# A smaller edge tile on 64x64 quadrants, mixer bursts joined in pairs, and their transposes moved: a change to a gated-attention and mixer kernel

## The chip, the cores and the metric

The kernel runs on one core of one Trainium2 chip. The metric is the device time of the whole program in microseconds (us), median of several runs. The engines are called as the profile calls them: PE is TensorE (PEld its weight loads), ACT is ScalarE, DVE is VectorE, POOL is GpSimd, SP is SyncE. SP only issues DMA transposes here.

## The reference, cut to what matters

There are 8 batches of S = 3136 rows; u and v have 256 columns, z has 64, the rank is 32.

```python
scores = (1.0 / S) * np.matmul(z, z.transpose(0, 2, 1))
x = u * np.matmul(np.maximum(scores, 0.0) ** 2, v)        # attention part
h = x.transpose(0, 2, 1) @ U @ V                           # low rank, along the rows
u2 = x + h.transpose(0, 2, 1)
out = u2 + np.maximum(u2 @ w_ch1, 0.0) @ w_ch2             # channel mixer, 256 -> 1024 -> 256
```

3136 rows are 24 tiles of 128 and one of 64, which is tile 24.

## The kernel before

The squared scores A are symmetric. So the kernel computes for each row tile j only 13 of 25 blocks (in `A[j]`) and gets the other 12 by a DMA transpose into a `strip`, issued four outputs ahead. An "output" is one row tile of the attention result. They are done in pairs that share a set of two PSUM banks, in the order 12, 13, ..., 24, 0, ..., 11; below, "output i" is the i-th place in this order, counted from 0, and tile 24 is output 12. Two 64-row matmuls at a time work on the two row halves of the array:

```python
def half(b, o, j, h, w, start, stop, **kw):
    ...
    mm(out=acc[t0][h][:, (o - t0) * D : (o - t0 + 1) * D],
       lhsT=w[halves[h]], rhs=v_both[b % 2][halves[h], j, :], ...)

def close_pair(b, o):
    ...
    nc.scalar.copy(out=both[:, :w], in_=banks[1][:, :w])
    nc.vector.tensor_tensor(out=both[:, :w], in0=banks[0][:, :w], in1=both[:, :w], op=ALU.add)
    nc.vector.tensor_tensor(out=x_at(b, t0, n), ..., op=ALU.mult)      # times u
```

Tile 24 has only 64 rows. Its z is stored twice over, so its 128 columns hold the same 64 rows twice, and half of its matmul work is wasted.

The mixer of batch b-1 runs inside the attention of batch b. There are 7 chunks of two to four row tiles. For each, `low_rank` puts a sum into the PSUM set that the open pair is not using, DVE adds it to x, and SP transposes the result into `ut`. A "burst" n then runs the up matmuls of chunk n (evicted by ACT with relu) and the down matmuls of chunk n-1:

```python
def low_rank(b, c, ps=None):
    ps = spare() if ps is None else ps          # the set that no open pair uses
    ... mm(...)                                  # four matmuls
    nc.vector.tensor_tensor(out=q, in0=split(ps[h]...), in1=q, op=ALU.add)   # twice
    transpose(out=ut..., in_=x...)               # SP queue

# the loop over the outputs of one batch, cut
burst_at = dict(zip((2, 4, 6, 8, 10, 13, 15, 17), range(NC + 1)))
z_load, z_double, z_half, z_turn = (1, 5, 7, 11) if b else (None, 9, 11, 13)
ahead = dict(zip((1, 2, 4, 6, 8, 10, 13), range(NC)))
for i in range(begin, NT):
    fill = [...]                                 # scores, spread over the output's matmuls
    if i == z_turn:     turn_z(b + 1, ((0, FIRST),))      # z of the next batch, SP queue
    if i == z_turn + 1: extend_z()                        # a DVE copy of what was turned
    main = attend_steps(b, o)
    if b and i in ahead:
        main.insert(NT * 2 // 5, lambda c=ahead[i]: low_rank(b - 1, c))      # step 10 of 25
    _spread(main, fill)
    if i + AHEAD < NT:  turn(b, turns(i + AHEAD))         # a strip, SP queue
    ...
    if b and i in burst_at:
        up, down = bursts[burst_at[i]]
        run(_merge(down, up))
```

`turn_z` overwrites z, so it can only start after the last score of the running batch (output 10 before).

Of the kernel before, what the change touches and what calls it, by code (L numbers as in the profile page):

```python
# [10 lines left out]
ALU = mybir.AluOpType  # L11
# [3 lines left out]
def _ceil_div(a, b):  # L15
    return (a + b - 1) // b
# [15 lines left out]
def _merge(*lists):  # L32

    keyed = [
        ((i + 0.5) / len(part), n, s)
        for n, part in enumerate(lists)
        for i, s in enumerate(part)
    ]
    return [s for _, _, s in sorted(keyed, key=lambda e: e[:2])]
# [3 lines left out]
def kernel(  # L43
# [11 lines left out]
    nc = tc.nc  # L55

    B, S, D = u.shape
# [4 lines left out]
    NT = _ceil_div(S, P)  # L62
    NF = S // P
# [8 lines left out]
    FIRST = HALF  # L72
# [22 lines left out]
    halves = [slice(h * ROWS, (h + 1) * ROWS) for h in range(2)]  # L95
# [5 lines left out]
    def spare():  # L101

        return sets[(opened[0] + (0 if acc else 1)) % 2]
# [4 lines left out]
    mm = nc.tensor.matmul  # L108
# [9 lines left out]
    v_both = [persist.tile([P, NT, D], BF16, name=f"v{k}") for k in range(2)]  # L118
# [4 lines left out]
    def turns(i):  # L123
        return (FIRST + i) % NT
# [4 lines left out]
    def col(t):  # L129
        return place(t) * P  # L130
# [10 lines left out]
    NC = len(chunks)  # L141
# [7 lines left out]
    def x_at(b, t, n=1):  # L149

        c, k = offset[t]
        return group(b, c)[:, :, k : k + n, :].rearrange("p a t c -> p t a c")

    def split(ap):
        return ap.rearrange("p (t a c) -> p t a c", a=ND, c=P)
# [32 lines left out]
    def extend_z():  # L188
        nc.vector.tensor_copy(out=zT[:, NT:, :], in_=zT[:, :HALF, :])
# [114 lines left out]
    acc = {}  # L304
    u_tiles = {}

    def pair_of(o):
        first = 0 if o < FIRST else FIRST
        stop = FIRST if o < FIRST else NT
        t0 = o - (o - first) % 2  # L310
        return t0, min(2, stop - t0)
# [11 lines left out]
    def open_pair(b, o):  # L323
        acc[pair_of(o)[0]] = sets[opened[0] % 2]
        opened[0] += 1

    def block(b, o, j):
        k = (o - j) % NT
        return A[j][:, k * P : (k + 1) * P] if k <= HALF else strips[b, o][:, NT - 1 - k, :]
# [12 lines left out]
    def close_pair(b, o):  # L342
        t0, n = pair_of(o)
        banks, u_sb = acc.pop(t0), u_tiles.pop((b, t0))
        w = n * D
        both = both_pool.tile([P, 512], FP32, name="both")
        nc.scalar.copy(out=both[:, :w], in_=banks[1][:, :w])  # L347
        nc.vector.tensor_tensor(  # L348
            out=both[:, :w], in0=banks[0][:, :w], in1=both[:, :w], op=ALU.add
        )  # L350
        nc.vector.tensor_tensor(  # L351
            out=x_at(b, t0, n),
            in0=split(both[:, :w]),
            in1=u_sb[:, :n, :].rearrange("p t (a c) -> p t a c", c=P),
            op=ALU.mult,
        )

    def after(b, o):

        t0, n = pair_of(o)  # L360
        i = place(t0) + n
        return (b, turns(i)) if i < NT else (b + 1, turns(0))

    def attend_steps(b, o):
        t0, n = pair_of(o)
        last = t0 + n - 1
        js = [(o - k) % NT if k < NB else (o + k - HALF) % NT for k in range(NT)]
        js.remove(NF)

        def step(i):  # L370
            if i == 0 and o == t0:
                open_pair(b, o)
                if after(b, o)[0] < B:
                    load_u(*after(b, o))
            if i < NT - 1:
                w = block(b, o, js[i])
                end = i == NT - 2
                half(b, o, js[i], 0, w, i == 0, end and o > t0)
                half(b, o, js[i], 1, w, i == 0 and o == t0, end)
            elif o == t0:  # L380
                half(b, o, NF, 0, block(b, o, NF), False, True)
                if o < last:
                    half(b, o + 1, NF, 1, block(b, o + 1, NF), True, False)
            if i == NT - 1 and o == last:
                close_pair(b, o)

        return [lambda i=i: step(i) for i in range(NT)]
# [26 lines left out]
    def low_rank(b, c, ps=None):  # L414

        ts = chunks[c]
        ps = spare() if ps is None else ps
        where = [(0, 0), (1, 0)] if len(ts) == 2 else [(0, 0), (0, 1), (1, 0), (1, 1)]
        order = sorted(zip(where, ts), key=lambda e: (e[0][1], e[0][0]))
        for (h, k), t in order:  # L420
            mm(  # L421
                out=ps[h][:, k * D : (k + 1) * D],
                lhsT=V_bf[halves[h], col(t) : col(t) + P],
                rhs=t1[b][halves[h], :],
                start=True,
                stop=True,
            )
        n = len(ts)
        x = group(b, c)
        dst = x.rearrange("p a t c -> p t a c")  # L430
        for h in range(2):
            ks = [k for (g, k), _ in zip(where, ts) if g == h]
            k0 = len(ks) * h if n == 2 else 2 * h
            q = dst[:, k0 : k0 + len(ks)]
            nc.vector.tensor_tensor(out=q, in0=split(ps[h][:, : len(ks) * D]), in1=q, op=ALU.add)  # L435
        ut = ut_pool.tile([P, ND * 512], BF16, name="ut")
        ut = ut[:, : ND * n * P].rearrange("p (a w) -> p a w", a=ND)
        transpose(
            out=ut.rearrange("p a (t c) -> p (a t) c", c=P),
            in_=x.rearrange("p a t c -> p (a t c)"),  # L440
        )
        uT[c] = ut
# [211 lines left out]
    own_at = {i: [] for i in range(NT)}  # L654
    for i, j in enumerate(range(LEAD + NG - 1, NT)):
        own_at[i].append((j, 0, NB))
    for j, i in enumerate((6, 7, 8, 9, 10, 10, 4, 2, 9, 8, 7, 6)):
        own_at[i].append((j, 0, FIRST - j))


# [11 lines left out]
    def run(steps):  # L672
        for s in steps:
            s()
# [4 lines left out]
    late = []  # L679
    for b in range(B):  # L680
        more = b + 1 < B
        begin = 0 if b else 2 * NG
        bursts = bursts_of(b - 1) if b else []
        burst_at = dict(zip((2, 4, 6, 8, 10, 13, 15, 17), range(NC + 1)))
        z_load, z_double, z_half, z_turn = (1, 5, 7, 11) if b else (None, 9, 11, 13)
        soon = next_at if b else next_first
        v_at = (1, 3, 4, 5, 7, 8, 10, 11, 12) if b else (8, 9, 10, 12, 14, 15, 16, 17, 18)
        v_at = dict(zip(v_at, V_PARTS))
        ahead = dict(zip((1, 2, 4, 6, 8, 10, 13), range(NC)))
        first = []  # L690
        if b == 0:
            for j, k1 in [(NT - 1, NB)] + [(j, NB if j < 3 else FIRST - j) for j in range(FIRST)]:
                first += score_steps(j, 0, k1)
        for i in range(begin, NT):
            o = turns(i)
            fill = []
            if b == 0:
                if i < z_turn:
                    n = _ceil_div(len(first), z_turn - i)
                    fill, first = first[:n], first[n:]  # L700
            else:
                fill = [s for key in own_at[i] for s in score_steps(*key)]
            if more:
                fill += [s for key in soon[i] for s in score_steps(*key)]
                if i == z_load:
                    load_z(b + 1, WHOLE)
                if i == z_double:
                    double_z(b + 1, WHOLE)
                if i == z_half:
                    turn_z(b + 1, ((FIRST, NF),))  # L710
                if i == z_turn:
                    turn_z(b + 1, ((0, FIRST),))
                if i == z_turn + 1:
                    extend_z()
                if i in v_at:
                    load_v(b + 1, v_at[i])
            main = attend_steps(b, o)
            if b and i in ahead:
                main.insert(NT * 2 // 5, lambda c=ahead[i]: low_rank(b - 1, c))
            _spread(main, fill)  # L720
            if i + AHEAD < NT:
                turn(b, turns(i + AHEAD))
            elif more:
                turn(b + 1, turns(i + AHEAD - NT))
            if b == 0 and i in weights:
                weights[i]()
            if b and i == 0:
                rank(b - 1)
            if b and i in burst_at:
                up, down = bursts[burst_at[i]]  # L730
                if not more and burst_at[i] >= NC - 1:
                    late += up + (down if burst_at[i] == NC else [])
                    up, down = [], (down if burst_at[i] < NC else [])
                run(_merge(down, up))


    last = bursts_of(B - 1)
# [5 lines left out]
    for c in range(NC + 1):  # L743
        up, down = last[c]
        if c + 2 < NC:
            up = up[:1] + [lambda c=c: low_rank(B - 1, c + 2, other)] + up[1:]
# [30 lines left out]
```

## Time and profile before

The median was 1065.91 us. The profiled run spans 1063.6 us.

| what | value | read from |
|---|---|---|
| PE busy, DVE, ACT | 95%, 49%, 57% | page, busy times |
| one batch, start to start of the rank matmuls | 126.83 us | timeline of PE |
| a slot: 2 matmuls of 64 rows x 256 columns, or one full-array of 256 | 109 ns | timeline of PE |
| excess over these slots in one batch | 5.4 us, once 5.8 and once 7.1 | worked out from matmul starts |
| a switch between 64-row and full-array matmuls | 0.09 to 0.10 us | worked out from matmul starts |

"Excess" is the time from one matmul start to the next on the same part of the array minus the slot (109 ns for 256 columns, 216 ns for 512).

The page's busy times and the chain that ended last:

```profile
PE 1010.7 (95%) x13829; PEld 791.3 (74%) x13829; DVE 525.3 (49%) x937; ACT 611.4 (57%) x814; POOL 178.7 (17%) x332
...
PE 81%; DVE 7%; ACT 5%; issue 3%; DMA 2%; POOL 1%; SPq 0%; POOLq 0%; ACTq 0%; DVEq 0%
```

PE is the bottleneck, and DMA is 2% of the chain: in the steady batches PE waits for a transfer only once (1.7 us, for a `ut`, in the one long period). Three lines of the waits (who waited for whom: us in total, times, longest) say the same:

```profile
DVE zT L189 <- DMA zT<-z_bf: 13.6, 2, 10.7
...
PE ps L421 <- DVE both L348: 8.3, 28, 0.4
...
PE ps L455 <- DMA ut<-x_bf: 4.3, 2, 2.7
```

L421 is the low-rank sum waiting for its PSUM set. L189 is the DVE copy of z; both its waits are in the first batch. The mixer waited for a `ut` only twice, once in the tail.

The timeline of PE shows tile 24 (start, duration, instruction): 24 slots, 2.63 us to the next output at 442.28.

```profile
439.65 1.47 PE L333 MATMUL ps<-v,A 64*128 64x256 bf16 x24
440.96 1.47 PE L333 MATMUL ps<-v,strip 64*128 64x256 bf16 x24
```

The timeline of the SP queue around the turning of z in the same batch:

```profile
431.19 1.23 SPq L438 DMA_TRANSPOSE ut<-x_bf  x1
432.52 1.48 SPq L295 DMA_TRANSPOSE strip<-A  x1
434.08 3.42 SPq L184 DMA_TRANSPOSE zT<-z_bf  x1
437.59 4.84 SPq L295 DMA_TRANSPOSE strip<-A  x2
```

### The profile page before, as it was taken

The numbers are of one execution on the slowest core, as the hardware profiler recorded it, in microseconds if no ns is written. First come the engines' busy times: TensorE is split into PE (matmuls) and PEld (weight loads), VectorE is DVE, ScalarE is ACT, GpSimd is POOL, SyncE is SP. The second block draws the span as 40 slices with busy tenths as digits, with TensorE's granted clock in tenths as the row PEclk, the third lists the DMA queues.
The fourth block names the chain that finished last, engine by engine and source line by source line (L and its number), as shares of the span: only waits on it lengthen the run. The fifth ranks groups of instructions, "written<-read, shape, count | busy, mean of one in ns | idle before, by whom it ended". The sixth has DMA issues, their size and how long they took to land.

```text
span 1063.6 us, 31097 instructions
## 1 busy us (share of the span) xinstructions
PE 1010.7 (95%) x13829; PEld 791.3 (74%) x13829; DVE 525.3 (49%) x937; ACT 611.4 (57%) x814; POOL 178.7 (17%) x332
## 2 busy tenths in 40 slices
PE   5879999999999999999999999999899999999896
PEld 4667777787777867788677877788677787778564
DVE  4858554465544654456543555436444465432331
ACT  5857555566645665466655665646665566541253
POOL 4122112111121111211121121211112110111011
PEclk9999999999999999999999999999999999999998
DMA  9999989779897998959899898987989797588231
GB/s 173 183 195 179 174 165 173 168 159 171 167 164 158 174 173 170 179 139 163 162 174 178 152 170 163 165 183 145 173 155 172 158 170 136 125 149 162 62 100 64
DMA packets 417174, 168.71 MB, mean 159 GB/s; under 512 B 392768, under 2 KB 402640, under 8 KB 417040
## 3 DMA queue, kind: packets, MB, share of 16 engines
q1 hardware_dynamic: 386464, 96.77, 56.9%
q0 software_dynamic: 30576, 69.96, 27.1%
q8 instruction: 108, 1.77, 0.7%
q14 instruction: 26, 0.21, 0.1%
HBM read 61.88 MB, written 25.69 MB: 82 GB/s over the span
## 4 chain that ended last, share of the span: by engine, by line
PE 81%; DVE 7%; ACT 5%; issue 3%; DMA 2%; POOL 1%; SPq 0%; POOLq 0%; ACTq 0%; DVEq 0%
PE ps L333 43%; PE ps L486 16%; PE ps L455 15%; PE ps L260 6%; ACT A L273 3%; DVE x_bf L435 3%; DVE both L348 2%; DVE A L275 2%; DMA zT<-z_bf 1%; PE ps L401 1%; DVE x_bf L351 1%; ACT both L347 1%; PE ps L421 1%; ACT relu L462 1%; DMA ut<-x_bf 1%
## 5 line engine op out<-in xcount | busy, mean ns | idle before, releaser
L273 ACT ACTIVATE A<-ps 128x832 bf16<-128x832 f32 (+8 forms) x469 | 351.7, 763 | 176.4 <-PE ps L260 170.6
L333 PE MATMUL ps<-v,A 64*128 64x256 bf16 x5064 | 358.6, 271 | 5.7 <-DVE x_bf L435 2.3
L275 DVE TENSOR_TENSOR A<-A 128x832 bf16<-128x832 bf16 (+8 forms) x469 | 240.3, 524 | 209.8 <-ACT A L273 206.8
L333 PE MATMUL ps<-v,strip 64*128 64x256 bf16 x4612 | 319.9, 270 | 0.0
L462 ACT ACTIVATE relu<-ps 128x1024 bf16<-128x1024 f32 (+2 forms) x224 | 203.1, 916 | 186.0 <-PE ps L455 186.0
L333 PEld LDWEIGHTS <-A 64*128 64x128 bf16 x5064 | 251.7, 94 | 64.5 <-issue 27.1
L333 PEld LDWEIGHTS <-strip 64*128 64x128 bf16 x4612 | 233.2, 94 | 34.1 <-issue 0.2
L455 PE MATMUL ps<-ut,w_bf 128*128 128x512 bf16 (+2 forms) x896 | 204.4, 354 | 7.4 <-DMA ut<-x_bf 4.3
L486 PE MATMUL ps<-w_bf,relu 128*128 128x256 bf16 x1600 | 205.9, 273 | 1.0
L486 PEld LDWEIGHTS <-relu 128*128 128x128 bf16 x1600 | 153.8, 98 | 49.5 <-issue 9.3
L497 DVE TENSOR_TENSOR o_sb<-ps,x_bf 128x512 f32<-128x512 f32 (+1 forms) x104 | 69.7, 670 | 221.3 <-PE ps L486 221.3
L260 PE MATMUL ps<-zT 64*128 64x416 bf16 (+9 forms) x933 | 156.0, 318 | 18.4 <-DMA zT<-z_bf 15.8
L455 PEld LDWEIGHTS <-w_bf 128*128 128x128 bf16 x896 | 86.3, 98 | 65.6 <-issue 11.6
L317 POOL DMA_DIRECT2D u_sb<-in_u_dram x96 | 53.5, 558 | 474.4 <-DVE x_bf L351 436.0
L504 POOL DMA_DIRECT2D out_dram<-o_sb x96 | 52.4, 546 | 330.2 <-DVE o_sb L497 330.2
L348 DVE TENSOR_TENSOR both<-ps,both 128x512 f32<-128x512 f32 (+1 forms) x104 | 69.3, 666 | 55.4 <-ACT both L347 55.0
L347 ACT COPY both<-ps 128x512 f32<-128x512 f32 (+1 forms) x104 | 58.9, 567 | 63.0 <-PE ps L333 63.0
L260 PEld LDWEIGHTS <-zT 64*128 64x128 bf16 x933 | 53.0, 95 | 27.2 <-DMA zT<-z_bf 16.1
L435 DVE TENSOR_TENSOR x_bf<-ps,x_bf 128x512 bf16<-128x512 f32 (+1 forms) x112 | 65.4, 626 | 14.7 <-PE ps L421 14.6
L351 DVE TENSOR_TENSOR x_bf<-both,u_sb 128x512 bf16<-128x512 f32 (+1 forms) x104 | 69.8, 671 | 3.6
L195 POOL DMA_DIRECT2D v<-in_v_dram x61 | 34.1, 566 | 0.5 <-issue 0.5
L421 PE MATMUL ps<-t_sb,V_bf 64*128 64x256 bf16 x200 | 22.6, 273 | 9.9 <-DVE both L348 8.3
(33 smaller groups left out, 134.0 us busy)
## 6 DMA issues: line engine op xcount, KB each, us to landing
u_sb<-in_u_dram POOLq DMA_DIRECT2D x96, 256.0 KB, 3.5
out_dram<-o_sb POOLq DMA_DIRECT2D x96, 256.0 KB, 3.0
v<-in_v_dram POOLq DMA_DIRECT2D x57, 192.0 KB, 5.7
strip<-A SPq DMA_TRANSPOSE x196, 4.9
z_c<-in_z_dram POOLq DMA_DIRECT2D x7, 384.0 KB, 5.7
w_bf<-in_moe_w_ch_dram POOLq DMA_DIRECT2D x2, 512.0 KB, 8.5
u_sb<-in_u_dram POOLq DMA_DIRECT2D x16, 64.0 KB, 2.1
ut<-x_bf SPq DMA_TRANSPOSE x56, 3.4
```

What stands on the lines that cost most here:

```text
L260: mm(out=ps[:, k, :n], lhsT=zT[halves[k], j, :], rhs=zT_flat[halves[k], c : c + n], start=True, stop=True,)
L273: nc.scalar.activation(out=dst, in_=src, func=AF.Relu, scale=sc)
L275: nc.vector.tensor_tensor(out=dst, in0=dst, in1=dst, op=ALU.mult)
L333: mm(out=acc[t0][h][:, (o - t0) * D : (o - t0 + 1) * D], lhsT=w[halves[h]], rhs=v_both[b % 2][halves[h], j, :], start=start, stop=stop, **kw,)
L347: nc.scalar.copy(out=both[:, :w], in_=banks[1][:, :w])
L348: nc.vector.tensor_tensor(out=both[:, :w], in0=banks[0][:, :w], in1=both[:, :w], op=ALU.add)
L351: nc.vector.tensor_tensor(out=x_at(b, t0, n), in0=split(both[:, :w]), in1=u_sb[:, :n, :].rearrange("p t (a c) -> p t a c", c=P), op=ALU.mult,)
L435: nc.vector.tensor_tensor(out=q, in0=split(ps[h][:, : len(ks) * D]), in1=q, op=ALU.add)
L455: mm(out=ps[:, i, :w], lhsT=w1_bf[:, db, (hp + i) * P : (hp + i + 1) * P], rhs=uT[c][:, db, len(chunks[c]) * P - w :], start=(db == 0), st ...
L462: nc.scalar.activation(out=relus[c][:, hp : hp + 2, :w], in_=ps[:, :, :w], func=AF.Relu)
L486: mm(out=ps[:, k * D : (k + 1) * D], lhsT=relus[c][:, ht, q : q + P], rhs=w2_bf[:, ht, :], start=(ht == 0), stop=(ht == NH - 1),)
L497: nc.vector.tensor_tensor(out=o_sb[:p, :nk, :].rearrange("p t (a c) -> p t a c", c=P), in0=split(ps[:p, : nk * D]), in1=x_at(b, t, nk)[:p] ...
```

## The change

The intent: halve the matmuls of tile 24, halve the number of switches into and out of the mixer, and place the low-rank sums where their PSUM set is already free. Within a burst, up now comes before down. The core of the diff:

```diff
+        if o == NF:                                   # in close_pair: fold the two column halves
+            for r in range(2):
+                nc.scalar.copy(out=both[halves[r], w : 2 * w], in_=both[halves[1 - r], :w])
+            nc.vector.tensor_tensor(
+                out=both[:, :w], in0=both[:, :w], in1=both[:, w : 2 * w], op=ALU.add
+            )
 ...
+    def quarter(b, j, n, h):
+        c = n % 2
+        mm(
+            out=acc[NF][h][halves[c], :D],
+            lhsT=block(b, NF, j)[halves[h], halves[c]],
+            rhs=v_both[b % 2][halves[h], j, :],
 ...
-    for j, i in enumerate((6, 7, 8, 9, 10, 10, 4, 2, 9, 8, 7, 6)):
+    for j, i in enumerate((6, 7, 8, 9, 3, 5, 4, 2, 9, 8, 7, 6)):
 ...
-        burst_at = dict(zip((2, 4, 6, 8, 10, 13, 15, 17), range(NC + 1)))
-        z_load, z_double, z_half, z_turn = (1, 5, 7, 11) if b else (None, 9, 11, 13)
+        burst_at = {4: (0, 1), 8: (2, 3), 13: (4, 5), 17: (6, 7)}
+        z_load, z_double, z_half, z_turn = (1, 5, 7, 10) if b else (None, 9, 11, 13)
 ...
-        ahead = dict(zip((1, 2, 4, 6, 8, 10, 13), range(NC)))
+        ahead = dict(zip((2, 3, 6, 7, 10, 11, 14), range(NC)))
 ...
-                main.insert(NT * 2 // 5, lambda c=ahead[i]: low_rank(b - 1, c))
+                main.insert(14 if (i + (i > FIRST)) % 2 == 0 else 8, lambda c=ahead[i]: low_rank(b - 1, c))
 ...
-                run(_merge(down, up))
+                run(_merge(up, down))                 # for both bursts n of burst_at[i]
```

Two row tiles j share a slot: the even ones go to the first 64 output partitions, the odd ones to the other 64, and the two halves are added at the end.

More of the change, by code (lines that the diff above doesn't have):

```diff
@@ L355, in close_pair @@
             op=ALU.mult,
+        )
+    def quarter(b, j, n, h):
[4 more added lines that the diff above has]
+            rhs=v_both[b % 2][halves[h], j, :],
+            start=(n < 2),
+            stop=(n == (NT - 2 if c else NT - 1 - 2 * h)),
         )
@@ L374, in step @@
                     load_u(*after(b, o))
-            if i < NT - 1:
+            if o == NF:
+                if i < NT - 1 and i % 2:
+                    for n in (i - 1, i):
+                        for h in range(2):
+                            quarter(b, js[n], n, h)
+                elif i == NT - 1:
+                    quarter(b, NF, i, 0)
+            elif i < NT - 1:
                 w = block(b, o, js[i])
@@ L728 @@
                 rank(b - 1)
-            if b and i in burst_at:
-                up, down = bursts[burst_at[i]]
-                if not more and burst_at[i] >= NC - 1:
-                    late += up + (down if burst_at[i] == NC else [])
-                    up, down = [], (down if burst_at[i] < NC else [])
-                run(_merge(down, up))
+            for n in burst_at.get(i, ()) if b else ():
+                up, down = bursts[n]
+                if not more and n >= NC - 1:
+                    late += up + (down if n == NC else [])
+                    up, down = [], (down if n < NC else [])
+                run(_merge(up, down))
     last = bursts_of(B - 1)
```

## The prediction

> **What bounds the kernel now.** TensorE. The page shows PE busy 95% of 1063.6 us and 81% of the chain that ended last; ACT (57%) and DVE (49%) are no limits. The batches repeat every 126.83 us (start to start of the rank matmuls in the timeline; one period is 128.56). Matmul by matmul, the timeline shows slots of 109 ns for a pair of 64-row matmuls of 256 columns or a full-array one of 256, and 216 ns for 512. Over these slots, a period has only 4.0 us of excess:
> - low-rank sums (L421) waiting for a spare PSUM set: 1.84 us;
> - an output's opening (L333) waiting for a set that a low-rank sum still holds: 0.59 us;
> - entering and leaving 8 mixer bursts: 16 switches of 0.09 to 0.10 us, 1.5 us, and 0.3 us in two entries, where down waits for PSUM;
> - the first, up-only burst waiting for relu evictions (1.02 us each against 0.87 us of matmuls): 0.54 us.
>
> **What the change does, per period.**
> 1. Quadrants: output tile 24 takes 24 slots, 2.63 us. Four 64x64 matmuls at once need 12: -1.31 us. The rank matmuls (128x32) start as four every 100 to 110 ns, so I expect four per slot. The Trainium skill (TensorEngine Tiling, "Key Properties" and "Restrictions") says that a change of tiling mode drains the array and that column tiling loses the fast weight load; the trace agrees on the first (0.09 us per switch); that 64-column loads stay hidden is a guess. Two switches cost 0.19. Net -1.1. The added ACT copies (2 x about 0.37) and DVE add (about 0.42) lie behind the close, off the chain.
> 2. Double bursts: eight switches fewer, -0.76; entry stalls gone, -0.3; but burst 1 now follows the up-only burst at once: one more wait for an eviction, +0.25.
> 3. Low-rank sums: step 14 comes 1.5 to 1.9 us after the opening, the set is free at about 1.7 to 1.9. But two sums in adjacent outputs put 2.8 us more on DVE in 6.5 us, so the second sum and the next opening still wait 0.3 to 0.4 in places. Of 2.4 us I expect 1.1 to stay: -1.3.
> 4. z sooner: the last own scores are now in output 9, and the DVE copy that extends zT stands at the start of output 11, with no burst between. Turning z takes 3.4 to 8.0 us from issue to landing. DVE is in order, so it is blocked 1 to 2 us and the opening of tile 24 is late by about 0.6 (0 to 1.5), in six batches.
>
> Sum: about -2.6 us per batch, seven batches: -18.5. First batch: quadrants alone, broken by scores: -0.5. The single 1.8 us wait for ut in the long period probably goes: -1. The start and the tail of about 70 us are unchanged. All this is on the critical path, since PE is.
>
> **Predicted: 1045 us, 80% range 1037 to 1054.** Faster by over 2%: 0.46; within 2%: 0.53; slower: 0.01.
>
> **What would show it.** A period near 124.2 us. Quadrant matmuls in fours every 105 to 115 ns. Four burst entries and four exits of about 0.09 us. Stalls before low-rank sums under half of 1.84 us. A wait of DVE's zT copy for DMA in the steady batches, which has none before; then a late opening of tile 24.
>
> **What would make it wrong.** Quadrants not four at once (slots of 160 to 210 ns): +5 to +9 us. No waits on DVE or zT: 1036. The longer burst-free stretch (12 outputs instead of 10, DMA share already 0.94 there) making strips late: several us more.

## The result, and the profile after

The changed kernel takes 1052.58 us (four runs, 1050.61 to 1056.54), the kernel before 1066.2 us in the same rounds. The ratio is 0.9878, with a 95% interval of 0.9847 to 0.991. A ratio here is the mean time of one kernel's fast runs over that of the other's of the same rounds, so not quite the ratio of the medians. The profiled run spans 1050.1 us, 13.5 less than before. Note the scatter: 5.9 us between the changed kernel's runs, 2.3 us between those of before.

The line numbers move by 24 in the mixer: L421 is now L445 (low-rank matmul), L455 is L479 (up), L486 is L510 (down), L435 is L459. The page of the changed kernel:

```profile
PE 996.5 (95%) x13829; PEld 788.7 (75%) x13829; DVE 527.8 (50%) x945; ACT 616.8 (59%) x830; POOL 179.2 (17%) x332
...
PE 77%; DMA 10%; ACT 4%; issue 3%; DVE 3%; POOL 1%; SPq 0%; POOLq 0%; ACTq 0%; DVEq 0%
```

PE is busy 14 us less, as it should be. But the share of DMA in the chain that ended last went from 2% to 10%: transfers now set the pace in places. The waits of the changed kernel:

```profile
DVE zT L189 <- DMA zT<-z_bf: 22.3, 8, 11.7
...
ACT A L273 <- DMA strip<-A: 12.8, 5, 3.8
...
PE ps L479 <- DMA ut<-x_bf: 6.8, 9, 2.7
...
PE ps L367 <- DVE x_bf L459: 2.3, 6, 0.8
```

The line of low-rank sums waiting for `both` (8.3 us, 28 times before) has gone. But this view leaves out idle times under 150 ns, and it counts from the modelled ends of matmuls. By the matmul starts, the sums still wait 1.0 us in a period, where they waited 1.9, and the waits of an opening behind a sum (0.6) have gone. Three waits for DMA have come or grown: of the mixer for `ut`, of ACT for strips (before there was none of this kind), and of DVE for z in every batch that has a next one. The last line is tile 24 (L367) waiting for the adds of a low-rank sum, which stand on DVE behind the copy of z.

Tile 24, timeline of PE of the changed kernel: 1.54 us from its first matmul to the next output's at 429.84, where it was 2.63.

```profile
428.30 0.85 PE L367 MATMUL ps<-v,A 64*64 64x256 bf16 x24
428.98 0.82 PE L367 MATMUL ps<-v,strip 64*64 64x256 bf16 x24
429.64 0.27 PE L367 MATMUL ps<-v,A 64*64 64x256 bf16 x1
```

The SP queue of the changed kernel in the same batch:

```profile
422.08 1.61 SPq L184 DMA_TRANSPOSE zT<-z_bf  x1
425.84 1.24 SPq L462 DMA_TRANSPOSE ut<-x_bf  x1
427.17 4.15 SPq L295 DMA_TRANSPOSE strip<-A  x1
431.41 1.26 SPq L462 DMA_TRANSPOSE ut<-x_bf  x1
432.76 7.94 SPq L295 DMA_TRANSPOSE strip<-A  x3
```

Now z stands in front of the `ut` and the strip, six us before tile 24 opens. The strip issued at 427.17 then delays something else. Here is the chain that ended last in that window (start, duration, what):

```profile
426.63 0.54 PE ps L333 x10
427.17 8.50 DMA strip<-A
...
435.75 0.39 ACT A L273
436.15 0.04 issue
436.19 1.02 PE ps L479 x4
```

And the timeline of ACT of the changed kernel at the same place (the bracket is idle time and what ended it):

```profile
431.66 0.28 ACT L273 ACTIVATE A<-ps 128x128 bf16<-128x128 f32 x1
435.75 0.38 ACT L273 ACTIVATE A<-ps 128x256 bf16<-128x256 f32 x1 [3.82 <-DMA strip<-A]
436.03 1.02 ACT L486 ACTIVATE relu<-ps 128x1024 bf16<-128x1024 f32 x1
```

The 128x256 score belongs to the next batch. It overwrites row 1 of A and must wait until that row's strip has landed. Behind it in ACT's queue stand the relu evictions of the double burst that has begun meanwhile, and so PE stops inside the burst: in this batch for 1.68 us.

The excess over the slots, summed over the seven periods between the first and the eighth group of rank matmuls (882.93 us before, 868.05 us after), gives this account. All rows are worked out from the matmul starts of the two profiled runs, each start against the end of the slot before it on the same part of the array; "forecast" is the prediction's term times its number of batches.

| term | forecast, us | measured, us |
|---|---|---|
| tile 24: slots, and its two switches | -7.7 | -7.3 |
| low-rank sums and openings waiting for PSUM | -9.1 | -10.7 |
| burst switches, and entries waiting for PSUM or ACT | -7.4 | -8.3 |
| relu evictions at the first up burst | +1.8 | +2.4 |
| opening of tile 24 late, behind the copy of z on DVE | +3.6 | +3.1 |
| bursts waiting for `ut` (1.7 before, 4.3 after) | -1 | +2.6 |
| PE stopped in the burst by ACT waiting for a strip | none | +3.3 |
| up to the first rank matmuls (116.0 to 117.4 us) | -0.5 | +1.4 |
| after the last ones (64.7 and 64.6 us) | 0 | 0.0 |

The measured column adds up to -13.5, as much as lies between the two spans.

### The profile page after: what moved, and what is told of

It reads as the page before. It is cut to its first block, busy times and chain, and to the rows that moved or that the text cites. A ratio compares the mean times of both kernels' runs of the same rounds, so it can differ in the third digit from the quotient of the medians.

```text
span 1050.1 us, 31112 instructions
## 1 busy us (share of the span) xinstructions
PE 996.5 (95%) x13829; PEld 788.7 (75%) x13829; DVE 527.8 (50%) x945; ACT 616.8 (59%) x830; POOL 179.2 (17%) x332
## 4 chain that ended last, share of the span: by engine, by line
PE 77%; DMA 10%; ACT 4%; issue 3%; DVE 3%; POOL 1%; SPq 0%; POOLq 0%; ACTq 0%; DVEq 0%
PE ps L333 41%; PE ps L510 15%; PE ps L479 13%; PE ps L260 6%; DMA ut<-x_bf 4%; DMA strip<-A 3%; DMA zT<-z_bf 3%; ACT A L273 3%; PE ps L425 1%; ACT relu L486 1%; PE ps L445 1%; DVE A L275 1%; DVE both L348 1%; DVE x_bf L459 1%; PE ps L367 1%
## 5 line engine op out<-in xcount | busy, mean ns | idle before, releaser
L333 PE MATMUL ps<-v,A 64*128 64x256 bf16 x4864 | 335.7, 271 | 3.4 <-DVE both L348 2.0
L333 PE MATMUL ps<-v,strip 64*128 64x256 bf16 x4420 | 308.2, 269 | 0.0
L486 ACT ACTIVATE relu<-ps 128x1024 bf16<-128x1024 f32 (+2 forms) x224 | 202.6, 917 | 140.6 <-PE ps L479 140.6
L333 PEld LDWEIGHTS <-A 64*128 64x128 bf16 x4864 | 242.7, 94 | 44.2 <-issue 11.6
L333 PEld LDWEIGHTS <-strip 64*128 64x128 bf16 x4420 | 224.8, 94 | 30.5
L479 PE MATMUL ps<-ut,w_bf 128*128 128x512 bf16 (+2 forms) x896 | 203.5, 354 | 13.1 <-DMA ut<-x_bf 6.8
L510 PE MATMUL ps<-w_bf,relu 128*128 128x256 bf16 x1600 | 204.7, 273 | 0.0
L510 PEld LDWEIGHTS <-relu 128*128 128x128 bf16 x1600 | 156.1, 98 | 46.2 <-issue 0.8
L260 PE MATMUL ps<-zT 64*128 64x416 bf16 (+10 forms) x933 | 154.8, 318 | 20.9 <-DMA zT<-z_bf 18.3
L479 PEld LDWEIGHTS <-w_bf 128*128 128x128 bf16 x896 | 85.0, 98 | 79.2 <-issue 17.4
L459 DVE TENSOR_TENSOR x_bf<-ps,x_bf 128x512 bf16<-128x512 f32 (+1 forms) x112 | 65.4, 625 | 15.8 <-PE ps L445 15.8
L445 PE MATMUL ps<-t_sb,V_bf 64*128 64x256 bf16 x200 | 24.2, 273 | 3.3 <-DVE x_bf L459 1.1
```

Of the source, the lines that this page charges most:

```text
L260: mm(out=ps[:, k, :n], lhsT=zT[halves[k], j, :], rhs=zT_flat[halves[k], c : c + n], start=True, stop=True,)
L333: mm(out=acc[t0][h][:, (o - t0) * D : (o - t0 + 1) * D], lhsT=w[halves[h]], rhs=v_both[b % 2][halves[h], j, :], start=start, stop=stop, **kw,)
L459: nc.vector.tensor_tensor(out=q, in0=split(ps[h][:, : len(ks) * D]), in1=q, op=ALU.add)
L479: mm(out=ps[:, i, :w], lhsT=w1_bf[:, db, (hp + i) * P : (hp + i + 1) * P], rhs=uT[c][:, db, len(chunks[c]) * P - w :], start=(db == 0), st ...
L486: nc.scalar.activation(out=relus[c][:, hp : hp + 2, :w], in_=ps[:, :, :w], func=AF.Relu)
L510: mm(out=ps[:, k * D : (k + 1) * D], lhsT=relus[c][:, ht, q : q + P], rhs=w2_bf[:, ht, :], start=(ht == 0), stop=(ht == NH - 1),)
```

## The experiments

The theories, by letter. L: each `ut` is issued only two outputs ahead of its burst and lands too late. S: z turned sooner stands in the way of `ut` in the SP queue and blocks DVE. Q: a strip between the two `ut` of a pair holds up the second. B: the DMA engines are nearly full. Formed on the way: Z, what counts is that z stands early in the SP queue; W, ACT waits for strips. The twelve kernels ran in four sets (4, 4, 3 and 1), each beside fresh runs of the kernel before, whose medians were 1064.61, 1067.66, 1066.43 and 1066.07 us. Each edit is against the changed kernel unless the heading says otherwise.

### Turning z later again

```diff
-        ... z_turn = (1, 5, 7, 10) if b else ...
+        ... z_turn = (1, 5, 7, 11) if b else ...
```

> The changed kernel with one part undone: the second half of z is turned at output 11 again, not 10. Theory S (z turned sooner stands ahead of the transposes ut in the SP queue and blocks DVE, so ut 4 and 5 come late): the waits of TensorE for ut in the double burst at output 13 go, about 4 us less than the changed kernel (1048.5). Theory L (ut is issued only two outputs ahead, too short a lead for a landing of 5 us): the waits stay, within 2 us of the changed kernel (1051 to 1055).

Measured: 1095.8 us, ratio 1.0306 (1.0264 to 1.0348). This is 43 us slower than the changed kernel; neither theory had it, and S fell with the wrong sign. The SP queue of this kernel:

```profile
442.23 1.24 SPq L462 DMA_TRANSPOSE ut<-x_bf  x1
443.56 4.05 SPq L295 DMA_TRANSPOSE strip<-A  x1
447.66 2.46 SPq L184 DMA_TRANSPOSE zT<-z_bf  x1
```

And its timeline of PE:

```profile
446.23 0.94 PE L333 MATMUL ps<-v,A 64*128 64x256 bf16 x14
452.49 0.24 PE L260 MATMUL ps<-zT 64*128 64x64 bf16 x2 [5.32 <-DMA zT<-z_bf]
```

One output later in the program means that z is issued behind a `ut`, which waits for its DVE adds, and behind a strip whose issue takes 4.05 us. That is 3.0 us after tile 24 opened (444.7), where the changed kernel issues it 6.2 us before. PE waits 5.32 us at the first score of output 13 here, and 5.2 to 6.4 us in each of the six batches that have a next one. The periods are 132.4 us in the mean of these six, against 125.2 in the changed kernel.

The wait costs more than itself. The granted clock falls to half for 3.4 or 6.8 us once in each of these periods (the clock record of this trace; the mean is 0.975 against 0.992), and slots of 109 ns become 213. The Trainium skill says so (TensorE: Matmul & The Clock Gate, Part 1): the clock gate halves the clock after about one idle window of 3.4 us. The traces agree on the long waits, and the halved stretches of the steady batches last 3.4 or 6.8 us. They do not agree on 3.4 us as the least: in the changed kernel waits under 2 us leave the clock alone, but in the run with the first scores at output 14, below, two stops of 2.3 to 2.5 us of missing work halved it, and one of 2.5 us with the sums spread did not.

### The low-rank sums one output earlier

```diff
-        ahead = dict(zip((2, 3, 6, 7, 10, 11, 14), range(NC)))
+        ahead = dict(zip((1, 2, 5, 6, 9, 10, 14), range(NC)))
```

> The changed kernel with every low-rank sum but the last one output earlier (outputs 1, 2, 5, 6, 9, 10, 14), so that each ut has one output more to land. Theory L: most of the 7.4 us in which bursts wait for ut go, 1046 to 1048. Theory S, or that DMA is simply full: little change, 1051 to 1054.

Measured: 1095.95 us, ratio 1.029 (1.027 to 1.031). The waits for `ut` did go in the steady batches (2.7 us left, all in the tail). But the `ut` of output 9 now precedes z in the SP queue again. Its chain that ended last:

```profile
444.40 7.62 DMA zT<-z_bf
...
452.04 0.04 DVE zT L189
...
452.51 0.69 DVE both L348
...
453.25 1.67 PE ps L333 x14
```

DVE stood 8.3 us at its copy of z, the close of the pair before stood behind it, and the next opening on PE waited 5.8 us. So L was not refuted: its gain was buried under the same accident as in the first experiment. In both runs a later z in the SP queue goes with a loss of 43 us, most of it at the opening of tile 24 or of output 13 and in the halved clock behind it.

### The quadrants alone, on the schedule of before

```diff
+        if o == NF:             # in close_pair, as in the change
+    def quarter(b, j, n, h):    # as in the change
+            if o == NF:         # in attend_steps, as in the change
```

> The kernel before with the quadrants of tile 24 alone, the schedule untouched. If quadrants give their 12 slots: 1.1 us per period less, seven periods, 1057 to 1059, less what a wait in the first batch gives back. If the time saved turns into a wait further on: 1063 to 1066.

Measured: 1064.73 us, ratio 0.9998 (0.9983 to 1.0013). Nothing is left of the gain. In one steady period tile 24 saves 1.1 us, but the sum at output 13 now waits 0.34 us for PSUM, and the burst behind it 0.67 us beyond the switch. The shorter tile 24 brings both of them nearer to its close. The sum, at step 10 of output 13, starts at 445.5 us, when the first DVE add of that close has ended (445.06 to 445.48 in this run) and its PSUM set is free. The close then goes on with two ACT copies and a DVE add that are new, to 447.24 on DVE, and the adds of the sum stand behind them (from 447.30); the burst at 448.1 waits for these:

```profile
PE ps L510 <- DVE x_bf L459: 4.0, 7, 0.6
```

The prediction had the new copies and the add off the chain; on this schedule they are on it. The changed kernel has no sum at output 13.

### The changed kernel without the quadrants

```diff
-            if o == NF:      # in the steps, and in close_pair
+            if False:
```

> The changed kernel with tile 24 as before (128 columns twice over), the rest of the change in place. If the parts add up: 8 us more than the changed kernel, 1060. If the shorter tile 24 only brings the double burst at output 13 to a ut that has not landed: 1054 to 1057, and the waits for ut in that burst get shorter by as much.

Measured: 1057.67 us, ratio 0.9923 (0.9902 to 0.9945). Against the changed kernel this is 5 us more (0.45% by the ratios, give or take 0.4), so of the 7.3 us of tile 24 about 5 arrive as time. This lies between the two expectations, nearer to the second: the profile shows no wait of bursts at output 13 (0 us, after 3.3), while the openings of tile 24 are late as before.

### Strips issued behind the second ut of a pair

```diff
-            if i + AHEAD < NT:
+            if b and i in (2, 6, 10):
+                held.append(turns(i + AHEAD))     # issued after low_rank of output i + 1
+            elif i + AHEAD < NT:
                 turn(b, turns(i + AHEAD))
```

> The changed kernel with the strip transpose at the end of outputs 2, 6 and 10 issued after the ut of the low-rank sum of the next output, so that each pair of ut stands together in the SP queue; no work is added or taken away. Theory Q (a strip whose issue takes 3 to 4 us stands between the two ut of a pair): TensorE's waits for ut in mid-burst go and those at the entry do not grow, 1046 to 1049. Theory B (the DMA engines are full and any order lands as late): 1051 to 1055.

Measured: 1085.39 us, ratio 1.0182 (1.0142 to 1.0222), over 30 us above either expectation. It was this run that showed theory W. The mixer's waits for `ut` did not shrink (9.2 us, after 6.8), so Q fell. The wait of ACT for strips nearly tripled:

```profile
ACT A L273 <- DMA strip<-A: 35.8, 6, 6.9
```

Delaying the strip of output 14 by one output makes the next batch's score of row 1 wait longer, and PE stands 3.7 to 4.7 us inside the burst at output 13 in five of six periods, with the halved clock after it. The more the strip is delayed, the more the burst loses: 12.8 us of ACT's wait gave 1052.6 us, 35.8 gave 1085.4.

### Without the loads of v

```diff
-                if i in v_at:
+                if i in v_at and b == 0:
```

> The changed kernel without the loads of v from the second batch on (the result is wrong on purpose; matmuls and dependencies of the other tiles stay), which takes away nine of the 192 KB transfers per period. Theory B (DMA bandwidth): transposes land sooner, waits for ut gone, 1043 to 1047. Theory Q (order in the queue alone): 1050 to 1054.

Measured: 1039.63 us, ratio 0.9737 (0.9709 to 0.9764). Its output is wrong, which doesn't matter for the time. The median landing of a `ut` falls from 5.0 to 3.4 us, the waits at burst entries go, of those inside the burst one of 0.6 us is left, and the periods are 123.4 to 124.6 us. So B holds in this sense: with fewer transfers the new waits go (DMA share 0.92 in a period of the changed kernel, 0.86 in this one). That DMA is nearly full does not make them by itself: the run called Both, below, keeps every transfer, has a share of 0.91, and has no wait for a `ut` or a strip in its steady batches. Where each transfer stands decides whether and where somebody waits.

### The new steps of the sums alone, on the kernel before

```diff
-                main.insert(NT * 2 // 5, ...
+                main.insert(14 if (i + (i > FIRST)) % 2 == 0 else 8, ...
```

> The kernel before with the low-rank sums at the new steps (14 in the first output of a pair, 8 in the second), at the old outputs and with the single bursts. If the stall for a spare PSUM set is a loss of TensorE in its own right: 1.3 to 1.8 us per period less, 1053 to 1057. If it only hides a wait that comes later (the DMA transposes of z at output 13): 1063 to 1066.

Measured: 1072.74 us, ratio 1.0046 (1.0019 to 1.0073): neither expectation, it is slower. The stalls before the sums have gone altogether, but with single bursts the sum of output 4, 6 or 8 is followed by a burst in the same output, whose down matmuls need the same PSUM set. Timeline of PE of this kernel:

```profile
394.46 0.71 PE L486 MATMUL ps<-w_bf,relu 128*128 128x256 bf16 x5 [1.10 <-DVE x_bf L435]
```

and of its DVE, where the adds that free the set stand:

```profile
393.13 1.28 DVE L435 TENSOR_TENSOR x_bf<-ps,x_bf 128x512 bf16<-128x512 f32 x2
```

Three such entries per period cost 1.07 to 1.27 us each, switch included. A later sum is a gain only if no burst follows it closely. The first batch holds no sums, so its instructions are those of before; it took 117.65 us here and 116.0 there. In the run with the double bursts alone, next, whose first batch is again that of before, it took 119.16 us. So the +1.4 us of the first batch in the account above is within what the same code shows, and is not put down to the change.

### The double bursts alone, on the kernel before

```diff
-        burst_at = dict(zip((2, 4, 6, 8, 10, 13, 15, 17), range(NC + 1)))
+        burst_at = {4: (0, 1), 8: (2, 3), 13: (4, 5), 17: (6, 7)}
 ...
-                run(_merge(down, up))
+                run(_merge(up, down))                 # for both bursts n of burst_at[i]
```

> The kernel before with the four double bursts alone: sums at the old outputs and step, tile 24 as before, z turned at output 11, own scores as before. If the burst that stood behind output 10 was what hid the turning of z (theory Z): TensorE waits for zT at output 13 in every period, with the clock halved after it, 1085 to 1100. If fewer switches are a gain by themselves: 1.1 us per period less, 1057 to 1060.

Measured: 1103.97 us, ratio 1.0351 (1.0323 to 1.038). As theory Z said: PE waits for z at output 13 in every period that has a next batch, 3.8 to 4.6 us, and the clock is halved after (the line below holds the first batch's two waits too, 16.7 us; before it was 15.8, 2, 9.6).

```profile
PE ps L260 <- DMA zT<-z_bf: 41.8, 8, 10.3
```

The burst that stood behind output 10 was what had hidden the turning of z. The double bursts took it away; turning z one output sooner, and ending the own scores at output 9, puts it back.

### The sums spread out again

```diff
-        ahead = dict(zip((2, 3, 6, 7, 10, 11, 14), range(NC)))
+        ahead = dict(zip((1, 2, 4, 6, 8, 10, 13), range(NC)))
```

> The changed kernel with the low-rank sums at the outputs of before (1, 2, 4, 6, 8, 10, 13), still at the new steps and with double bursts: no two sums of a double burst in adjacent outputs except the first, and each ut earlier. Theory L (lead too short): waits for ut go, and the second sum no longer waits on DVE, 1043 to 1047. Theory Z (what counts is that z stands ahead of the ut transposes in the SP queue, as the two slow runs suggest): no loss either, since the ut of output 10 is behind z; slower than 1060 would mean that z is held up by something else.

Measured: 1054.21 us, ratio 0.9862 (0.9807 to 0.9917), with runs from 1044.74 to 1057.77: inconclusive by its time. Its profile is clearer. The waits for `ut` are gone but for the tail, as L said; ACT's wait for strips is larger than in the changed kernel (12.8):

```profile
ACT A L273 <- DMA strip<-A: 17.4, 5, 5.6
```

Of its first six periods three were 124.1 to 124.2 us and one was 130.3, with a stall of 3.3 us in the burst at output 13 and the clock halved.

### The next batch's first scores behind the burst

```diff
-    next_at = ahead_of([max(NB, FIRST + j) for j in range(FIRST)], ...
+    next_at = ahead_of([max(NB + 1, FIRST + j) for j in range(FIRST)], ...
```

> The changed kernel with the next batch's first two short scores (rows 0 and 1) moved from output 13 to output 14, behind the double burst, and nothing else. Theory W (their eviction on ACT must wait until the strips of outputs 13 and 14 have been read by DMA; ACT is in order, so the relu evictions of the burst stand behind it, and TensorE stalls in the burst, 0.4 to 1.7 us per period): the mid-burst stalls at output 13 go, the wait of ACT for strips goes, 1047 to 1050. Theory L alone (those stalls are ut landing late): 1051 to 1054.

Measured: 1053.62 us, ratio 0.9871 (0.9847 to 0.9895). The wait of ACT for strips has gone, and with it the stalls inside the burst, as W said. The time has not moved, against W: the waits have moved to the burst entries and to the opening of tile 24 (1.8 us once).

```profile
PE ps L479 <- DMA ut<-x_bf: 9.3, 8, 2.7
...
PE ps L367 <- DVE x_bf L459: 3.2, 6, 1.7
```

The longest of each (2.5 us at a burst entry, and the 1.8 at tile 24) were followed by 3.4 us of halved clock. An estimate: 3.4 us at half clock lose 1.7, so 3.4 us of this run's time are lost to the clock alone, and the two periods concerned took 128.2 us.

### Both

The two edits above together.

> The same with the low-rank sums at the outputs of before (1, 2, 4, 6, 8, 10, 13), so that each ut has longer to land. If W and L are the two causes and add up: periods of 124.2 us all through and no scatter between runs, 1043 to 1046. If the scatter of the kernel with spread sums (1044.7 to 1057.8) has another cause, it stays.

Measured: 1046.43 us (1045.66 to 1048.1), ratio 0.9812 (0.9794 to 0.9831). This is the fastest correct kernel: 6 us under the changed one and 20 under the one before. Its waits for DMA, of the same kinds as above:

```profile
DVE zT L189 <- DMA zT<-z_bf: 22.9, 8, 10.6
...
PE ps L479 <- DMA ut<-x_bf: 2.7, 1, 2.7
```

There is no wait of ACT for strips, and the one for `ut` is in the tail. Five periods are 124.10 us and one is 124.04; the scatter of the runs is down to 2.4 us, that of the kernel before. The four kernels make a square:

| | first scores at output 13 | at output 14 |
|---|---|---|
| sums in adjacent outputs | 1052.58 | 1053.62 |
| sums spread | 1054.21 | 1046.43 |

The four come from three sets of runs, so their ratios to the kernel before are the safer comparison: 0.9878 and 0.9871 above, 0.9862 and 0.9812 below. The later scores alone gain nothing; the spread sums alone are undecided (one run of four was as fast as both together); both gain 0.7%, give or take 0.4. Why one makes the other's wait larger is argued, not shown: in each case the same transfers had to pass in the same time, and the one left in front of PE grew.

### z of the first batch sooner, on top of both

```diff
-        ... else (None, 9, 11, 13)
+        ... else (None, 9, 11, 12)
```

> The same, and in the first batch the second half of z is turned at output 12, not 13, so that it stands in front of one more strip in the SP queue. TensorE waits 8.7 us for it in the changed kernel, at half clock after. If the place in the queue sets that wait: 3 to 4 us less than the run before this one. If the transfer itself is slow there: within 1 us.

Measured: 1046.69 us, ratio 0.9819 (0.9795 to 0.9843), the same as without the edit. PE's wait for z in the first batch was still 6.7 us (7.5 us in the run without this edit, within the scatter of the first batch). But the edit hardly moved z: it was issued at 71.49 us instead of 71.86, since the strips in front of it took longer, and it landed 8.7 us after its issue instead of 9.1. So this run does not show what an earlier issue would give. What sets the 9 us stays open.

## Why the prediction was right or wrong

The time, 1052.58 us, lies within the range of 1037 to 1054, near its upper end, and the class given the best chance (within 2%) came true. Neither says much: that class had 0.53 against 0.46, and the range of 17 us was wide enough to hold a sum that was 7 us off. The gain was 13.6 us where 21 was forecast.

- What bounds the kernel, the slots and the excess: right. Every gain of PE time was sized to within a fifth: tile 24 (-7.7 forecast, -7.3 measured), the sums (-9.1, -10.7; of 2.6 us in a period 1.1 stay, as forecast), the bursts (-7.4, -8.3). That all of it lay on the critical path was right only while nothing else waited: alone, the quadrants gave 0, the steps of the sums +5 us and the double bursts +38. Quadrants in fours every 105 to 115 ns: right; 428.30 to 429.64 us is twelve groups of four in 1.34 us.
- "one more wait for an eviction, +0.25": right in kind, too small; it was 2.4 us in seven periods, 0.35 each.
- "z sooner" as a loss: DVE waits for z in the steady batches, as forecast, and tile 24 opens late: by 0.8, 0.9 and 1.4 us in three of the six batches and hardly in the others, 0.5 in the mean, where 0.6 (0 to 1.5) was forecast. That is right, size included. But the step was only half read. It counted what the new place of z costs and not what the old place would have cost. Without it the changed kernel takes 1095.8 us. The prediction saw that no burst stood between the last score and the copy any more, and did not ask what the old `z_turn` would then do.
- "The single 1.8 us wait for ut in the long period probably goes: -1": wrong in sign. The lead of a `ut` had been two outputs and a burst for most chunks; for the bursts at outputs 4 and 8 it became two outputs or one, with no burst between. Its landing went from 3.4 us (median) to 5.0, and the sum allowed for neither. Entries of these two bursts now wait for it in five of the seven periods.
- The stall inside the burst at output 13, +3.3 us, had no term in the sum. The prediction named strips coming late as a danger, in the stretch of 12 outputs. They came late elsewhere, at output 14's strip, and reached PE not through a matmul but through ACT's queue.
- The first batch: not attributable; the same code varies by 3.2 us there (116.0, 117.65 and 119.16).

So the steps that failed are the terms for waits on DMA: forecast at -1 us, measured at +5.9 us (2.6 and 3.3). This alone is the 7 us that were missing; the first batch (1.9 us apart) and the evictions (0.6) are about made up by the sums, the bursts and the opening of tile 24. The run called Both shows it from the other side: with these waits gone, the period is 124.10 us, where the prediction had 124.2, and the time 1046.43, where it had 1045. That it fits so closely is partly luck: there the sums and openings wait 1.6 us in a period, 0.5 more than forecast, and tile 24 opens on time, 0.5 sooner than in the changed kernel.

## What to carry to other kernels

When a burst of other work is moved, list what was hidden behind it: here the turning of z sat behind one burst, and the double bursts alone made the kernel 38 us slower. In an in-order queue, ask for each wait who stands behind it: a score that waits for a transfer stops the evictions behind it, and a transpose behind a transpose waits for the first one's issue. If two repairs each do nothing, try them together before dropping them.

## What the Trainium skill lacked or had wrong

- TensorEngine Tiling, "Key Properties", says that a change of tiling mode drains the array, without a cost. Here each switch between 64-row and full-array matmuls, and into and out of 64x64 quadrants, costs 0.09 to 0.11 us.
- TensorEngine Tiling, "Restrictions", says that column tiling disables the fast weight load. That page gives no number for what it costs: here a 64x64 load took 106 to 107 ns against 94 ns for a 64x128 one, and it stayed hidden; four quadrants ran in a slot of 109 ns.
- DMA: Bandwidth & Descriptors, "DMA Transpose (X-bar)", does not tell how long the issue of a transpose holds its queue; elsewhere the page has cycle counts for it, in a comparison of trn3 with earlier generations, but no spread. Here issuing a strip of 128x12x128 held the SP queue for anything from 1.27 to 5.9 us (kernel before, median 1.48; changed kernel 1.27 to 5.7, median 2.03), and one output's difference in the order of that queue moved the program by 43 us.
- TensorE: Matmul & The Clock Gate states that ACT and DVE queues are strictly first in, first out; the trace agrees (a 3.82 us wait of one small score held back the relu evictions behind it, and PE with them for 1.68 us). No page warns that the wait then shows on PE under another name.
- TensorE: Matmul & The Clock Gate, Part 1, puts the halving at one idle window or more, about 3.4 us. Here, in the run with the first scores at output 14, stops of PE of 2.3 to 2.5 us were enough twice, and one of 2.5 us with the sums spread was not; so a wait well under 3.4 us can cost clock too.
